# Attention and token MLP on one core: masked Q evacuation in place of padded Q weights, two extra matmuls a period, new load order and tail

## Chip, cores and metric

One core of one Trainium2 chip. The metric is device time of the whole kernel in microseconds (us), median of several executions; lower is better. Launch-to-launch spread of the kernel before is about 0.3%.

## The reference

`x` is [1, 2048, 512] bf16. Layernorm gives `xn`; the result is `x + A(xn) + B(xn)`.

```python
def A(x, wqkv, wo):                 # 32 heads of 16
    q, k, v = split(x @ wqkv)
    p = softmax((q @ k.T) * 16 ** -0.5)
    return (p @ v) @ wo

def B(x, w1, b1, w2, b2):           # MLP over the tokens, F = 1376
    h = layernorm(x)
    u = gelu(h.T @ w1 + b1)
    return (u @ w2 + b2).T
```

The scores have 32 x 2048 x 2048 elements, and each of them needs an exp.

## The kernel before

Work is recorded into one stream for each engine by a Python loop over 512 *periods*. A period handles one group: 128 keys of four heads against 512 queries. Sixteen periods (all 2048 keys) are a *block*; 32 blocks cover 8 groups of heads and 4 blocks of queries. In each period TensorE does 4 score matmuls (q times k), 4 PV matmuls (p times v) of an earlier period, and a few *extra* matmuls of everything else; ScalarE does two exps. To *evacuate* is to copy a matmul's result out of PSUM, the memory that TensorE writes to, into SBUF, the working memory. Code and diffs here are shortened (an instruction stands for the call that records it, `...` for what is left out); the whole kernel is printed below.

```python
while True:
    if period < NGRP:
        score_group(period)                 # TensorE: 4 matmuls, 32 rows each (0.61 us together at half clock)
        exp_pair(2 * period)                # ScalarE: [128, 1024], PSUM -> SBUF
        exp_pair(2 * period + 1)
    ...                                     # PV of a period before; after 16 of them the block's epilogue
    budget = EXTRA_BUDGET if period < END else 1e9        # 3.0
    while bank_q:                           # one spare PSUM bank (EX_BANK), so one task at a time
        tk = bank_q[0]
        ...
        if tk.req == 0.0:                   # a step without matmuls (evacuation): ends the period's extras
            tk.advance()
            if period < END: break
            continue
        if budget >= tk.req or budget >= EXTRA_BUDGET:
            budget -= tk.req
            tk.advance()
        else: break
```

Tasks: `kt` (K projections, 4 chunks of 4 matmuls), `qt` (Q projection of one block, 4 matmuls), `ut` (first MLP product, 11 tasks of 16 matmuls, then gelu, whose tanh runs on ScalarE), `yt` (second product, 16 tasks of 11), `op` (output projection, 8 matmuls for 128 tokens).

Heads lie 16 rows apart and the score matmuls' tiles 32 (32*128 in their profile rows). So the 32 heads' Q weights were copied into a padded array with zeros, once for even and once for odd heads:

```python
def qt_block(b, bk, evac_eng="dve"):
    qb, G = divmod(b, NG)
    for ct in range(NCT):
        matmul(bank(bk), lhsT=wq_pad[:, ct, G, :], rhs=xnT[:, ct, 512*qb:512*(qb+1)], ...)
    evac(evac_eng, QT[:, b % NQS, :], bank(bk), ...)
```

GpSimd filled `wq_pad` (4 memsets, 8 copies) between its layernorm steps in the start stage.

The softmax here doesn't subtract the row's maximum and nothing guards it: scores larger than these inputs give would overflow.

## Time and profile before

| | before |
|---|---|
| median of 12 | 1041.68 us (1040.19 to 1043.09) |
| span of the profiled run | 1040.5 us |
| ScalarE busy / TensorE busy | 93% / 86% |
| start to first exp | 43.8 us |
| first exp to end of last exp | 981.6 us |
| end of last exp to end | 15.1 us |
| mean granted TensorE clock | 0.705 |

ScalarE's exps are the chain, so only start, tail and the breaks between exps can be saved. The views are shown and worked out in the prediction; one row of the page is added here. It gives the granted TensorE clock in 40 slices of 26 us, in tenths of full speed:

```profile
PEclk9966887897889999955557755555555955555558
```

From slice 18 on the row is mostly at 5, half clock (0.57 on the mean from 450 to 1000 us). This is the part of the kernel where only attention is left.

### The profile page before, as it was taken

The numbers are of one execution on the slowest core, as the hardware profiler recorded it, in microseconds if no ns is written. First come the engines' busy times: TensorE is split into PE (matmuls) and PEld (weight loads), VectorE is DVE, ScalarE is ACT, GpSimd is POOL, SyncE is SP. The second block draws the span as 40 slices with busy tenths as digits, with TensorE's granted clock in tenths as the row PEclk, the third lists the DMA queues.
The fourth block names the chain that finished last, engine by engine and source line by source line (L and its number), as shares of the span: only waits on it lengthen the run. The fifth ranks groups of instructions, "written<-read, shape, count | busy, mean of one in ns | idle before, by whom it ended". The sixth has DMA issues, their size and how long they took to land.

```text
span 1040.5 us, 11570 instructions
## 1 busy us (share of the span) xinstructions
PE 895.5 (86%) x4833; PEld 210.2 (20%) x4896; DVE 295.0 (28%) x476; ACT 967.2 (93%) x1065; POOL 75.8 (7%) x116
## 2 busy tenths in 40 slices
PE   5777888888889999999988898888998899888995
PEld 2211222221222222211112211111111211111111
DVE  6654433343332223322211222221022222102214
ACT  3698999999999999999999999999999999999994
POOL 6431000000000000000000000000000000000000
PEclk9966887897889999955557755555555955555558
DMA  5020201011012111100000000000000000000000
GB/s 141 19 43 21 48 21 41 21 27 30 1 29 53 35 29 43 28 0 1 1 1 11 11 1 1 1 1 1 0 1 6 16 1 1 1 1 1 1 1 20
DMA packets 54372, 18.31 MB, mean 18 GB/s; under 512 B 49200, under 2 KB 53808, under 8 KB 54320
## 3 DMA queue, kind: packets, MB, share of 16 engines
q1 hardware_dynamic: 54320, 17.58, 7.1%
q8 instruction: 38, 0.62, 0.2%
q14 instruction: 14, 0.11, 0.0%
HBM read 15.47 MB, written 2.10 MB: 17 GB/s over the span
## 4 chain that ended last, share of the span: by engine, by line
ACT 77%; PE 15%; DVE 4%; issue 1%; POOL 1%; DMA 1%; ACTq 0%; SPq 0%
ACT pT L597 77%; PE ps L588 4%; PE ps L383 3%; PE ps L607 2%; PE ps L468 2%; DVE stats L323 1%; DVE big L338 1%; PE ps L400 1%; POOL mv L329 1%; PE ps L514 1%; DMA x_sb<-in_A_x_dram 1%; PE ps L369 1%; ACT ga_sb L483 1%; DVE mv L325 0%; POOL mv L327 0%
## 5 line engine op out<-in xcount | busy, mean ns | idle before, releaser
L597 ACT ACTIVATE pT<-ps 128x1024 bf16<-128x1024 f32 x1024 | 946.3, 1242 | 32.8 <-PE ps L588 32.7
L588 PE MATMUL ps<-QT,KT 32*128 32x512 bf16 x2048 | 483.5, 513 | 97.2 <-ACT pT L597 62.0
L607 PE MATMUL ps<-pT,V 128*32 128x512 bf16 x2048 | 264.0, 517 | 2.2 <-DVE OT L546 1.9
L588 PEld LDWEIGHTS ps<-QT,KT 32*128 32x128 bf16 x2048 | 93.5, 96 | 509.5 <-ACT pT L597 460.2
L546 DVE COPY OT<-ps 128x512 f32<-128x512 f32 x32 | 22.1, 692 | 436.9 <-PE ps L607 436.8
L559 DVE RECIPROCAL denb<-denb 128x128 f32<-128x128 f32 x128 | 110.3, 915 | 0.9
L569 POOL TENSOR_TENSOR oT<-OT,denb 128x512 bf16<-128x512 f32 x31 | 39.3, 1267 | 881.6 <-DVE denb L559 881.6
L607 PEld LDWEIGHTS ps<-pT,V 128*32 128x32 bf16 x2048 | 52.9, 99 | 171.2 <-issue 167.9
L468 PE MATMUL ps<-big,w1blk 128*128 128x512 bf16 (+1 forms) x165 | 54.5, 436 | 2.8 <-issue 2.1
L383 PE MATMUL ps<-xnT,wq_pad 128*128 128x512 bf16 x101 | 43.2, 558 | 7.8 <-issue 7.8
L495 PE MATMUL ps<-gT,w2blk 128*128 128x512 bf16 (+1 forms) x165 | 47.3, 387 | 2.3 <-issue 1.9
L514 PE MATMUL ps<-wo_pad,oT 128*128 128x512 bf16 x115 | 36.0, 415 | 2.0 <-issue 1.8
L377 DVE CAST QT<-ps 128x512 bf16<-128x512 f32 x31 | 21.4, 692 | 36.2 <-PE ps L383 36.2
L500 DVE SCALAR_TENSOR_TENSOR big<-ps,x_sb 128x512 f32<-128x512 f32 x16 | 11.1, 691 | 66.8 <-PE ps L495 66.8
L473 DVE TENSOR_SCALAR u_sb<-ps,b1col 128x512 f32<-128x512 f32 (+1 forms) x11 | 8.2, 750 | 73.4 <-PE ps L468 73.4
L527 DVE TENSOR_TENSOR osb<-ps,big 128x512 bf16<-128x512 f32 x16 | 11.1, 691 | 58.0 <-PE ps L514 55.4
L376 ACT ACTIVATE xnT<-ps 128x512 bf16<-128x512 bf16 x16 | 9.5, 594 | 16.1 <-PE ps L348 16.1
L554 DVE STREAM_SHUFFLE denb<-OT 128x512 f32<-128x512 f32 x32 | 23.1, 722 | 0.0
L369 PE MATMUL ps<-xnT,wqkv_sb 128*128 128x512 bf16 x61 | 17.9, 412 | 3.8 <-DVE KT L377 3.2
L348 PE MATMUL ps<-ident,big 128*128 128x128 bf16 x64 | 7.0, 237 | 15.9 <-DVE big L338 15.9
L468 PEld LDWEIGHTS ps<-big,w1blk 128*128 128x128 bf16 (+1 forms) x176 | 14.1, 106 | 29.1 <-issue 21.4
L383 PEld LDWEIGHTS ps<-xnT,wq_pad 128*128 128x128 bf16 x128 | 12.9, 121 | 27.7 <-issue 24.5
(44 smaller groups left out, 209.6 us busy)
## 6 DMA issues: line engine op xcount, KB each, us to landing
w1blk<-in_B_w_dram SPq DMA_DIRECT2D x10, 512.0 KB, 4.1
w2blk<-in_B_w_dram SPq DMA_DIRECT2D x16, 320.0 KB, 3.3
out_dram<-osb SPq DMA_DIRECT2D x16, 128.0 KB, 1.7
wqkv_sb<-in_A_wqkv_dram SPq DMA_DIRECT2D x1, 1536.0 KB, 6.6
x_sb<-in_A_x_dram SPq DMA_DIRECT2D x3, 512.0 KB, 8.5
wo_pad<-in_A_wo_dram SPq DMA_DIRECT2D x8, 64.0 KB, 2.0
w2blk<-in_B_w_dram SPq DMA_DIRECT2D x16, 24.0 KB, 1.8
w1blk<-in_B_w_dram SPq DMA_DIRECT2D x1, 384.0 KB, 4.0
```

Of the source, the lines that this page charges most:

```text
L369: sc.add("pe", lambda e, ct=ct: e.matmul(bank(bk), lhsT=wqkv_sb[:, ct, D + 128 * T: D + 128 * T + 128], rhs=xnT[:, ct, 512 * c:512 * (c + ...
L383: sc.add("pe", lambda e, ct=ct: e.matmul(bank(bk), lhsT=wq_pad[:, ct, G, :], rhs=xnT[:, ct, 512 * qb:512 * (qb + 1)], start=(ct == 0), sto ...
L468: sc.add("pe", lambda e, st=st: e.matmul(bank(EX_BANK)[0:m, :], lhsT=w1blk[:, slot, st, 0:m], rhs=h_sb[:, st, :], start=(st == 0), stop=(s ...
L495: sc.add("pe", lambda e, ft=ft, m=m: e.matmul(bank(EX_BANK), lhsT=w2blk[0:m, slot, ft, :], rhs=gT[0:m, ft, :], start=(ft == 0), stop=(ft = ...
L514: sc.add("pe", lambda e, G=G: e.matmul(bank(EX_BANK), lhsT=oT[:, par, G, 128 * sti:128 * (sti + 1)], rhs=wo_pad[:, G, :], start=(G == 0), ...
L546: sc.add("dve", lambda e: e.tensor_copy(OT32[:, eb, :], bank(PV_BANK)), reads=[("bank", PV_BANK)], writes=[("OT32", eb)])
L554: sc.add("dve", lambda e: e.stream_shuffle(denb[:, eb, :], OT32[:, eb, :], [16] * 32), reads=[("OT32", eb)], writes=[("denb", eb, c) for c ...
L559: sc.add("dve", lambda e, cs=cs: e.reciprocal(denb[:, eb, cs], denb[:, eb, cs]), reads=[("denb", eb, c)], writes=[("denb", eb, c)])
L569: sc.add("pool", lambda e: e.tensor_tensor(oT[:, qb % 2, G, :], OT32[:, eb, :], denb[:, eb, :], ALU.mult), reads=[("OT32", eb)] + [("denb" ...
L588: sc.add("pe", lambda e, r=r, bk=bk: e.matmul(bank(bk), lhsT=KT[32 * r:32 * r + 32, T, 128 * kt:128 * (kt + 1)], rhs=QT[32 * r:32 * r + 32 ...
L597: sc.add("act", lambda e: e.activation(pT[:, buf, :], ps[:, s_ * 1024:(s_ + 1) * 1024], ACTF.Exp, scale=0.25), reads=[("bank", 2 * s_), (" ...
L607: sc.add("pe", lambda e, r=r, buf=buf, off=off: e.matmul(bank(PV_BANK)[32 * r:32 * r + 32, :], lhsT=V17[:, off:off + 32], rhs=pT[:, buf, 5 ...
```

## The change

Intent: halve the Q projection matmuls, spread the extra work more thinly, start earlier, and shorten the tail.

```diff
-EXTRA_BUDGET = 3.0
+EXTRA_BUDGET = 2.0
-        wq_pad = sb("wq_pad", [128, NCT, NG, 128], BF16)
+        qmask = sb("qmask", [128, 2], F32)        # 1 on 16 rows, 0 on 16; and the opposite
 ...
+        ld_x(0, 1); ld_x(1, 2); ld_w(2)            # V weights
+        ld_x(2, 4); ld_x(4, 8); ld_w(1)            # K weights
+        ld_x(8, 12); ld_x(12, 16); ld_w(0)         # Q weights   (before: x(0,1), all weights, the rest of x)
 ...
+        def qt_proj(qb, T, bk):                    # one projection for two blocks
+            for ct in range(NCT):
+                matmul(bank(bk), lhsT=wqkv_sb[:, ct, 128*T:128*(T+1)], rhs=xnT[...])
+            for e_ in range(2):
+                b = 8 * qb + 2 * T + e_
+                tensor_scalar(QT[:, b % NQS, :], bank(bk), qmask[:, e_:e_+1], None, ALU.mult)   # VectorE
 ...
-            ng = NG - 1 if lastqb else NG
+            ng = NG - 2 if lastqb else NG          # last query block: two groups are left for the tail
 ...
+        def tail_epilogue(b):
+            for sti in range(4): final_pre(qb, sti)            # group 6 into banks 0..3, under the shuffle
+            stream_shuffle(denb, bank(PV_BANK), [16] * 32)      # straight out of PSUM, no copy
+            recip_mult(0)                                       # reciprocal, multiply, final matmul
+            for c in range(1, 4):
+                recip_mult(c)
+                final_store(4 * qb + c - 1, c - 1)              # the store runs one chunk behind
+            final_store(4 * qb + 3, 3)
 ...
                     tk.advance()
+                    if tk.req == 0.0 and period < END:          # evacuate in the period of the last matmul
+                        tk.advance()
+                        break
```

## The prediction

> **What bounds the kernel now.** I read four views in this order: the page's chain of work that ended last with the costliest groups, ScalarE's own timeline, TensorE's timeline around one gap, and VectorE's timeline at the start and at the end.
>
> ```profile
> ACT 77%; PE 15%; DVE 4%; issue 1%; POOL 1%; DMA 1%; ACTq 0%; SPq 0%
> ...
> L597 ACT ACTIVATE pT<-ps 128x1024 bf16<-128x1024 f32 x1024 | 946.3, 1242 | 32.8 <-PE ps L588 32.7
> ...
> L383 PE MATMUL ps<-xnT,wq_pad 128*128 128x512 bf16 x101 | 43.2, 558 | 7.8 <-issue 7.8
> ```
>
> The exp on ScalarE (L597) is the chain. It ran 1024 times and was idle only 32.8 us, and all of that for scores (L588). TensorE's 86% busy share is therefore no bound by itself; what counts is where the scores come late. ScalarE's timeline shows that as breaks in its runs of exps:
>
> ```profile
> 514.39 29.44 ACT L597 ACTIVATE pT<-ps 128x1024 bf16<-128x1024 f32 x32 [0.86 <-PE ps L588]
> 544.68 12.94 ACT L597 ACTIVATE pT<-ps 128x1024 bf16<-128x1024 f32 x14 [0.86 <-PE ps L588]
> 558.05 1.94 ACT L597 ACTIVATE pT<-ps 128x1024 bf16<-128x1024 f32 x2 [0.43 <-PE ps L588]
> 560.54 44.10 ACT L597 ACTIVATE pT<-ps 128x1024 bf16<-128x1024 f32 x48 [0.55 <-PE ps L588]
> 605.50 29.44 ACT L597 ACTIVATE pT<-ps 128x1024 bf16<-128x1024 f32 x32 [0.86 <-PE ps L588]
> ```
>
> A run of 2 takes 1.94 and one of 32 takes 29.44, so the pitch is (29.44 - 1.94)/30 = 0.917 us, and 1024 of them cost 939. Each break costs its idle time plus 0.11 of drain (1.94 - 2 x 0.917). First exp at 43.78, last one done at 1025.4, span 1040.5: so 43.8 of start, 981.6 of exps (939, some 4.5 for the 11 tanh, the rest breaks) and 15.1 of tail. The breaks sort by what TensorE did just before them: early, up to 80 us, 3 of them, 3.0 us; in the stage of the first MLP product (80 to 295 us) 21 breaks, 15.3 us; from 450 us on 16 breaks of 0.86, each after a Q projection (L383), 16 x 0.96 = 15.4; and three pairs of 0.43 and 0.55, where output projections start, 3.5. Sum 37.
>
> Why they exist, seen at one of the pairs on TensorE:
>
> ```profile
> 162.40 1.46 PE L468 MATMUL ps<-big,w1blk 128*128 128x512 bf16 x3
> 163.79 0.61 PE L588 MATMUL ps<-QT,KT 32*128 32x512 bf16 x4
> 164.34 0.62 PE L607 MATMUL ps<-pT,V 128*32 128x512 bf16 x4
> 164.89 1.46 PE L468 MATMUL ps<-big,w1blk 128*128 128x512 bf16 x3
> ```
>
> This is the slow clock (granted 0.5). One period is 4 scores, 4 PV and the extras that the schedule slips in: 0.55 + 0.55 + 3 x 0.46 = 2.49 us, against 1.83 for the two exps that it feeds. At full clock the same three extras fit (no break from 300 to 450 us). With 4 extras, a Q projection, it is some 2.9: hence the 0.96 per Q projection.
>
> [...]in stretches of 0.5 us the granted clock rises at 560.40, 802.74 and 1014.37[...].
> [...]the layernorm's tensor_scalar takes 0.38 us alone and 1.01 while GpSimd clears wq_pad.
> [...]plain evacuation of 128x512 0.692 us, tensor_scalar of the same size (L473) 0.750. So a mask on the way out is nearly free.
>
> **The change, part by part.**
> *Q projection.* One projection now serves two blocks, and two masked evacuations on VectorE split it. Matmuls of this kind fall from 128 to 64, evacuations stay 32 (31 on VectorE before, all 32 now, 0.7 each, off the path). In the new order of instructions the projections stand in every second block; those in the long attention-only stretch, where the clock is slow, are 5 (blocks 19, 21, 23, 27, 29; those in 17 and 25 stand among output projections). 5 x 0.96 = 4.8 in place of 15.4: -10.6.
> *Two extras a period in place of three.* At slow clock: 0.55 + 0.55 + 2 x 0.46 = 2.03, that is 0.20 over the exps, and the first 0.12 is slack. [...]it should still wake the clock, [...]some 2.5 periods, 0.4 us a start in place of 1.2. [...]it stays warm. The MLP stage has 11 gaps of two empty periods in the new order. A gap puts the clock back[...] (I take 70%, before it was nearly always): 0.7 x (6 starts x 0.4 + 2 K projections x 1.5 + 3 Q projections x 1.1) = 6.1, plus 1.9 at its first block: 8.0 in place of 15.3, -7.3. Output projections: two starts of 0.4 and four short bursts at the end, 2.4 in place of 3.5, -1.1. I charge +0.7 for a second product that now and then falls cold on its one-extra period, and +0.8 because a Q projection now holds the extra bank for two evacuations (0.7 longer) before the next extras. Exp stage: -10.6 - 7.3 - 1.1 + 1.5 = -17.5.
> *Start.*
>
> ```profile
> 8.17 0.69 DVE L323 BATCH_NORM_STATS2 stats<-x_sb 128x6 f32<-128x512 bf16 x1 [4.37 <-DMA x_sb<-in_A_x_dram]
> ...
> 9.00 0.38 DVE L338 TENSOR_SCALAR big<-x_sb,mv 128x512 bf16<-128x512 bf16 x1
> ...
> 10.15 1.01 DVE L338 TENSOR_SCALAR big<-x_sb,mv 128x512 bf16<-128x512 bf16 x1
> ```
>
> The second x tile waited 4.37 behind 1536 KB of weights. It now goes ahead of them, and weights come in three parts in order of need: -4.3. Three memsets of wq_pad go (3 x 0.63 = 1.9 of VectorE), but TensorE is cold and saturated there, so I count 1.0 only. The last layernorm waits 3.6 us under the memset of wo_pad at 33.4; that memset stays where it is. Start: -5.3, first exp near 38.5.
> *Tail.*
>
> ```profile
> 1029.14 0.69 DVE L527 TENSOR_TENSOR osb<-ps,big 128x512 bf16<-128x512 f32 x1 [0.48 <-PE ps L537]
> 1029.75 0.68 DVE L520 TENSOR_TENSOR big<-ps,big 128x512 f32<-128x512 f32 x1
> ...
> 1032.32 0.69 DVE L527 TENSOR_TENSOR osb<-ps,big 128x512 bf16<-128x512 f32 x1 [0.70 <-PE ps L537]
> ```
>
> VectorE's chain from 1025.89 to 1038.16 is 12.27 us. Gone: the copy out of PSUM (0.74), the last residual add (0.6, now earlier) and four waits for the final matmul (0.48 + 3 x 0.70 = 2.58), since each store now follows the next reciprocal and multiply. Left: shuffle 0.75, four times 1.29, three stores at 0.61 and one of 0.69: 8.4, so -3.8; I take 3.7, as the last stores wait a little for the two output buffers (1.7 us from issue to landing). Two groups are left for the end in place of one, but the first of them is multiplied under the shuffle.
> Sum: 5.3 + 17.5 + 3.7 = 26.5, so 1041.75 - 26.5 = 1015.
>
> **The rivals.** (a) Two extras never wake the clock. [...]Then the MLP's 88 periods pay 0.2 each, 17.6, until some projection wakes it: about 1028. (b) Two extras wake it, but do not hold it, or the two evacuations and two-slot bank make new waits: +5 to +8, about 1022. (c) The gaps of the slow clock are only an accompaniment, and halving the Q projections gives nothing as the K projections' and evacuations' waits take their place: 1030. Against it: each break after 450 us has a Q projection before it and nothing else. (d) The memsets' full 1.9 is gained and gaps rarely cool the clock: 1009.
>
> **Range and chances.** Start and tail are well founded (9.0, give or take 1.5); the exp stage is 17.5 with some 6 either way, mostly downward through the clock. 8 in 10: 1008 to 1024. The line of 2% is 1020.9; (a), half of (b) and (c) lie beyond it. Faster 0.77, within 2% 0.22, slower 0.01.
>
> **What would show it.** Right: first exp at 38 to 39; breaks of 0.86 only in every second block after 450 us; at starts of two extras, two or three breaks near 0.2 and then a warm clock; no L520 add and no wait of 0.7 for TensorE in the tail, which is 11.4 us long. Wrong: a clock of 0.5 through the stage of the MLP with a break of 0.2 in each period; breaks with the release by the masked evacuation; or a first exp after 41.

## The result and the profile after

1019.03 us, median of 8 (1015.42 to 1020.05), against 1041.68. The ratio is 0.978 (95% interval 0.9769 to 0.9792). Ratios here are the mean time of one kernel's fast runs over that of the other's of the same rounds, so they are not quite the ratio of the quoted medians. The predicted time was 1015, the range 1008 to 1024.

Span 1018.1, that is 22.4 less. The same checkpoints of ScalarE's timeline, before and after:

| stretch | before | after | difference | predicted |
|---|---|---|---|---|
| start to first exp | 43.78 | 40.84 | -2.9 | -5.3 |
| first exp to exp 41 | 41.30 | 41.86 | +0.6 | 0 |
| exp 41 to exp 297 (first MLP product) | 254.1 | 249.2 | -4.9 | -7.3 |
| exp 297 to end of last exp | 686.2 | 675.2 | -11.0 | -10.2 |
| tail | 15.1 | 11.1 | -4.0 | -3.7 |

(Exp 297 of the kernel before has no break at it; its start is worked out as 293.34 + 50 x 0.917 from the break before it. The start differs from run to run; see a3. The -10.2 is the prediction's -10.6 for the Q projections, -1.1 for output projections, +1.5 of charges.)

From the page of the changed kernel:

```profile
PEclk9767898987788999997996855555555955555566
...
L619 ACT ACTIVATE pT<-ps 128x1024 bf16<-128x1024 f32 x1024 | 946.8, 1277 | 18.5 <-PE ps L610 16.8
...
L387 PE MATMUL ps<-xnT,wqkv_sb 128*128 128x512 bf16 x55 | 21.8, 530 | 2.8 <-issue 2.8
```

ScalarE's idle time before exps went from 32.8 to 18.5. By the clock record of the two traces, the scores that ended a break of over 0.15 us ran at half clock in 43 of 46 breaks before (30.1 of 32.2 us) and in 19 of 22 after (13.5 of 15.2). The projection group shows 55 matmuls against 101 (some records are missing in both: 64 and 128 were built). ScalarE's timeline, late part:

```profile
683.32 58.77 ACT L619 ACTIVATE pT<-ps 128x1024 bf16<-128x1024 f32 x64 [0.86 <-PE ps L610]
742.95 117.55 ACT L619 ACTIVATE pT<-ps 128x1024 bf16<-128x1024 f32 x128 [0.86 <-PE ps L610]
861.35 58.77 ACT L619 ACTIVATE pT<-ps 128x1024 bf16<-128x1024 f32 x64 [0.86 <-PE ps L610]
```

The runs between breaks are now mostly 64 or 128 exps long, two or four blocks, where most were 32. From 600 us on there are five breaks of 0.86, at blocks 19, 21, 23, 27 and 29, as foretold.

TensorE's timeline at the start of the first MLP task:

```profile
82.06 0.61 PE L610 MATMUL ps<-QT,KT 32*128 32x512 bf16 x4
82.60 0.62 PE L629 MATMUL ps<-pT,V 128*32 128x512 bf16 x4
83.15 1.03 PE L471 MATMUL ps<-big,w1blk 128*128 128x512 bf16 x2
84.11 0.61 PE L610 MATMUL ps<-QT,KT 32*128 32x512 bf16 x4
...
86.17 0.53 PE L610 MATMUL ps<-QT,KT 32*128 32x512 bf16 x4
```

Periods start at 82.06, 84.11 and 86.17: 2.055 us each at the slow clock (granted 0.5; 2.03 was predicted), and the clock rises to full at 86.5 (the 0.53 and the shorter matmuls that follow it). So two extras do wake it. The loss of 0.22 a period (2.055 against two exps of 0.917) need not show in the idle column: the drain of an exp (0.11) hides half of it, and the view doesn't split a run at an idle time as short as the rest (0.11). This row of ScalarE's timeline shows none, but the run is longer than its count allows:

```profile
99.92 18.93 ACT L619 ACTIVATE pT<-ps 128x1024 bf16<-128x1024 f32 x20
```

Twenty exps should take 19 x 0.917 + 1.02 = 18.44; the run took 0.49 more (the starts of two of its exps come 0.31 and 0.22 late; before the second, ScalarE idled 0.12). Whoever sums idle times misses this part.

### The profile page after: what moved, and what is told of

Its sections match the earlier page's. It is cut to its first block, busy times and chain, and to the rows that moved or that the text cites. A ratio compares the mean times of both kernels' runs of the same rounds, so it can differ in the third digit from the quotient of the medians.

```text
span 1018.1 us, 11428 instructions
## 1 busy us (share of the span) xinstructions
PE 860.1 (84%) x4770; PEld 197.2 (19%) x4832; DVE 294.5 (29%) x476; ACT 966.6 (95%) x1064; POOL 70.7 (7%) x110
## 4 chain that ended last, share of the span: by engine, by line
ACT 80%; PE 13%; DVE 4%; POOL 1%; issue 1%; DMA 0%; SPq 0%; ACTq 0%
ACT pT L619 79%; PE ps L610 4%; PE ps L629 2%; PE ps L387 1%; PE ps L471 1%; DVE stats L329 1%; PE ps L409 1%; DVE big L344 1%; PE ps L375 1%; POOL mv L335 1%; PE ps L517 1%; ACT ga_sb L486 1%; DMA x_sb<-in_A_x_dram 0%; PE ps L354 0%; DVE mv L331 0%
## 5 line engine op out<-in xcount | busy, mean ns | idle before, releaser
L619 ACT ACTIVATE pT<-ps 128x1024 bf16<-128x1024 f32 x1024 | 946.8, 1277 | 18.5 <-PE ps L610 16.8
L610 PE MATMUL ps<-QT,KT 32*128 32x512 bf16 x2048 | 463.6, 494 | 117.8 <-ACT pT L619 91.5
L629 PE MATMUL ps<-pT,V 128*32 128x512 bf16 x2048 | 257.7, 505 | 2.4 <-DVE OT L553 1.9
L565 DVE RECIPROCAL denb<-denb 128x128 f32<-128x128 f32 x124 | 107.0, 915 | 0.9
L471 PE MATMUL ps<-big,w1blk 128*128 128x512 bf16 (+1 forms) x160 | 56.7, 432 | 4.4 <-issue 2.9
L498 PE MATMUL ps<-gT,w2blk 128*128 128x512 bf16 (+1 forms) x160 | 54.1, 405 | 3.3 <-issue 1.9
L517 PE MATMUL ps<-wo_pad,oT 128*128 128x512 bf16 x105 | 38.5, 441 | 5.5 <-issue 3.2
L394 DVE TENSOR_SCALAR QT<-ps,qmask 128x512 bf16<-128x512 f32 x32 | 22.6, 747 | 18.9 <-PE ps L387 18.9
L387 PE MATMUL ps<-xnT,wqkv_sb 128*128 128x512 bf16 x55 | 21.8, 530 | 2.8 <-issue 2.8
L560 DVE STREAM_SHUFFLE denb<-OT 128x512 f32<-128x512 f32 x31 | 22.4, 723 | 0.0
L375 PE MATMUL ps<-xnT,wqkv_sb 128*128 128x512 bf16 x61 | 20.0, 458 | 2.6 <-DVE KT L383 1.5
L335 POOL TENSOR_TENSOR mv<-mv,mhalf 128x1 f32<-128x1 f32 x32 | 18.2, 568 | 2.7
L409 PE MATMUL ps<-wqkv_sb,xnT 128*128 128x512 bf16 x62 | 18.1, 419 | 0.1
```

The lines of the kernel that those rows point to most:

```text
L335: sc.add("pool", lambda e: e.tensor_tensor(mv[:, i, 2:3], mv[:, i, 1:2], mhalf[:], ALU.pow), reads=[("mv", i), ("mhalf",)], writes=[("mv", ...
L375: sc.add("pe", lambda e, ct=ct: e.matmul(bank(bk), lhsT=wqkv_sb[:, ct, D + 128 * T: D + 128 * T + 128], rhs=xnT[:, ct, 512 * c:512 * (c + ...
L387: sc.add("pe", lambda e, ct=ct: e.matmul(bank(bk), lhsT=wqkv_sb[:, ct, 128 * T:128 * (T + 1)], rhs=xnT[:, ct, 512 * qb:512 * (qb + 1)], st ...
L409: sc.add("pe", lambda e, ct=ct: e.matmul(bank(bk), lhsT=xnT[:, ct, 128 * t:128 * (t + 1)], rhs=wqkv_sb[:, ct, 2 * D:3 * D], start=(ct == 0 ...
L471: sc.add("pe", lambda e, st=st: e.matmul(bank(EX_BANK)[0:m, :], lhsT=w1blk[:, slot, st, 0:m], rhs=h_sb[:, st, :], start=(st == 0), stop=(s ...
L498: sc.add("pe", lambda e, ft=ft, m=m: e.matmul(bank(EX_BANK), lhsT=w2blk[0:m, slot, ft, :], rhs=gT[0:m, ft, :], start=(ft == 0), stop=(ft = ...
```

## The experiments

Twelve kernels, in three lots, each lot on one chip with its own runs of the kernel before (1044.02, 1042.0 and 1042.39 us). To compare I use ratios to the kernel before; one percent of it is 10.4 us. The 95% interval of a ratio is about 0.002 to either side, 2 us: by time alone, a difference of 2 us from the change (a3, a4, and nearly c1) isn't clear of noise, and the traces have to decide.

| run | edit to the changed kernel | median us | ratio to before | mean clock |
|---|---|---|---|---|
| the change itself | | 1019.03 | 0.978 | 0.74 |
| a1 | three extras | 1032.72 | 0.9899 | 0.689 |
| a2 | one projection a block | 1026.31 | 0.9847 | 0.767 |
| a3 | loads of before | 1022.3 | 0.9798 | 0.746 |
| a4 | tail of before (wrong result) | 1022.15 | 0.98 | 0.754 |
| c2 | tail of before, mended | 1025.41 | 0.9844 | 0.747 |
| b1 | + two idle matmuls a period | 1004.92 | 0.9646 | 0.961 |
| b2 | + the same from block 16 only | 1012.15 | 0.9711 | 0.938 |
| c1 | + one idle matmul a period | 1016.09 | 0.9755 | 0.81 |
| b3 | kernel *before* + two idle matmuls | 1011.7 | 0.9712 | 0.976 |
| b4 | clearing of wo_pad moved | 1015.65 | 0.9749 | 0.741 |
| c3 | b1 and b4 together | 1001.49 | 0.9614 | 0.962 |
| c4 | c3 + second layernorm in two steps | 997.24 | 0.9572 | 0.966 |

The theory: ScalarE's exps are the floor, and the breaks between them come from TensorE at half clock, where a period with two extra matmuls or more takes longer than two exps (2.055 us with two, against 1.83). The change gains by making fewer such periods. The rival: TensorE's amount of work, or waits for evacuations, make the breaks. One part of the change, that a task now evacuates in the period of its last matmul, was undone in no run.

### Undoing one part each

**a1, three extras.**

```diff
-EXTRA_BUDGET = 2.0
+EXTRA_BUDGET = 3.0
```

> The changed kernel with three extra matmuls a period again in place of two (all else kept). Theory (starts at the slow clock cost ScalarE 0.66 us a period with three extras and 0.22 with two): the eleven restarts of the first MLP product and the starts of the output projections cost about 0.6 us more each; about 1026 us, with breaks in pairs of 0.43 and 0.55 back in the profile. Rival (the cost of a restart does not depend on the number of extras[...]): within 1 us of 1019.

Measured: 12 us slower than the change by ratio (0.0119), nearly twice what I expected. Two causes are in ScalarE's timeline: the stage of the first MLP product (exp 41 to exp 297) alone is 7.5 us longer, 256.7 against 249.2, which is what I expected for all; the rest is late. The pairs of breaks are back, also at each short burst of output projections at the end:

```profile
974.16 1.94 ACT L619 ACTIVATE pT<-ps 128x1024 bf16<-128x1024 f32 x2 [0.43 <-PE ps L610]
976.65 7.44 ACT L619 ACTIVATE pT<-ps 128x1024 bf16<-128x1024 f32 x8 [0.55 <-PE ps L610]
984.52 1.94 ACT L619 ACTIVATE pT<-ps 128x1024 bf16<-128x1024 f32 x2 [0.43 <-PE ps L610]
987.01 9.27 ACT L619 ACTIVATE pT<-ps 128x1024 bf16<-128x1024 f32 x10 [0.55 <-PE ps L610]
```

And the MLP is done in block 12 in place of block 16, so the Q projections of blocks 13 and 15 fall into the stretch at half clock (breaks of 0.86 at 454.8 and 514.4 us). The rival is out, since the restarts of that stage cost what the theory said. So two extras do two things: restarts get cheaper (the 7.5 us), and the clock stays up longer since the work lasts longer (mean clock 0.74 in the change, 0.689 in a1).

**a2, one projection a block.**

```diff
-            for e_ in range(2):
+            for e_ in only:                      # (e_,): one masked evacuation a projection
...
-                    sched_list.append((P(b - 1, 1), 0, "qt", (qb, T)))
+                    for e_ in range(2): sched_list.append((P(b' - 1, 1), 0, "qt", (qb, T, e_)))
```

> The changed kernel, but each block projects its own Q again (four matmuls and one masked evacuation a block, so 128 projection matmuls in place of 64). Theory (every lone Q projection at the slow clock holds ScalarE up by 0.96): eleven or twelve more breaks of 0.86 in the attention-only stretch and one to three more earlier, some 12 us: about 1031 us. Rival (projections are hidden anyway and what helped was the rest): within 2 us of 1019.

Measured: 7.0 us slower by ratio (0.0067; its runs scatter from 1023 to 1029). After 515 us it has 12 breaks of 0.86 or so and one of 0.43, in place of 6 in all; eleven were to be added, seven were (blocks 18, 20, 22, 24, 26, 28 and 30). The direction is right, the size too large: with two extras the MLP lasts into block 16 here (542.6 us) and output projections follow, and the clock, at 1.0 but for one stretch from 326 to 579 us (slices 14 to 22 of its row are at 9), covers the projections of blocks 13 to 16.

**a3, the old loads.**

```diff
-        ld_x(0, 1); ld_x(1, 2); ld_w(2); ld_x(2, 4); ld_x(4, 8); ld_w(1); ld_x(8, 12); ld_x(12, 16); ld_w(0)
+        ld_x(0, 1); <all of wqkv in one transfer>; ld_x(1, 2); ld_x(2, 4); ld_x(4, 8); ld_x(8, 12); ld_x(12, 16)
```

> The changed kernel with the loads of before: the first x tile, then all weights in one transfer, then the rest of x. Theory: the first exp moves back by 3.2 us (the first VectorE evacuation of V was at 11.91 in the changed kernel and at 15.07 before), about 1022 us, first exp at 44. Rival (the gain at the start is from the removed clearing of the padded weights, not from the loads): first exp at 41 to 42.

Measured: first exp at 43.17 in place of 40.84. But the first exp moves from run to run with unchanged start code: 39.42 in a4, 40.69 to 40.87 in the change, b1, b2, c1 and c2, 41.15 in a1. The clock record shows a reason: the change has a stretch of half clock from 35.3 to 38.7 us, just after TensorE waited 3.1 us for VectorE, the other five from 40.69 up have one near there too, and a4 has none before its first exp. Neither have a3 and b3 (the start of the kernel before, 42.86). (The second slice of the clock row, 25 to 51 us, is at 7 or 8 in those six and at 9 in these three.) Like with like, the order of loads is worth 43.17 - 39.42 = 3.75 us, up to 0.7 of it a late landing in a3 (VectorE starts on tile 1 at 8.99, in b3 at 8.32), and nothing is seen of the rest (the removed filling of the padded weights, the first Q evacuation on VectorE). The exp stage was the same, 965.2 us against 966.2. By ratio it is 1.9 us.

**a4 and c2, the old tail.** In a4 I left the last output projections where the change puts them, in block 30. With one group more they then read a group that isn't written yet, in the program's order: the result was wrong (relative error 0.19). The timing of the tail isn't touched by that, but c2 repeats it with right results.

```diff
-            ng = NG - 2 if lastqb else NG
+            ng = NG - 1 if lastqb else NG
-            stream_shuffle(denb, bank(PV_BANK), ...)
+            epilogue_copy(b); stream_shuffle(denb, OT32[:, eb, :], ...)
-            (stores one chunk behind)
+            for c in range(4): recip_mult(c); final_store(4 * qb + c, c)
 c2 also:  last output projections from block 31, period 8 on, three extras there
```

> The changed kernel with the tail of before: copy out of PSUM first, one final group of matmuls, each store straight after its own multiply, one group more in the output projections of the last block. Theory: tail 4 us longer, from last exp to end 15.1 in place of 11.05, about 1023 us. Rival (the tail's gain is only that of the one residual add): 1 us longer.

> The old tail once more, now with right results: the last output projections start in block 31 as before the change, with three extras there, all residual adds ahead of the tail, then the copy out of PSUM and store after store. Theory: tail from last exp to end 14 to 15 us in place of 11.05, 1022 to 1023 us. Rival (the tail makes no difference as stores are hidden): 1019 us.

Measured: in a4 14.8 us from the last exp to the end, in c2 16.6, in the change 11.1. By ratio a4 is 2.1 us slower than the change and c2 6.7. (a4's profile is only 1.6 us longer, though its tail is 3.7 longer, as its first exp came 1.4 earlier, see a3, and its exp stage was 0.7 shorter.) In c2 the exp stage is 966.3, as in the change (966.2), and so is the first exp (40.87), so of the 5.6 us between the two profiles 5.5 are the tail; its last residual add stands in front of the copy and waits:

```profile
1009.22 0.69 DVE L523 TENSOR_TENSOR big<-ps,big 128x512 f32<-128x512 f32 x1 [1.94 <-PE ps L517]
1009.83 0.68 DVE L553 COPY OT<-ps 128x512 f32<-128x512 f32 x1
```

So c2's tail is 1.5 us worse than that of the kernel before, and I take 4 us, the difference of the two traces, for the tail's worth. In the changed kernel's tail, the stores follow without any wait for TensorE, and the last two run back to back:

```profile
1012.69 0.68 DVE L530 TENSOR_TENSOR osb<-ps,big 128x512 bf16<-128x512 f32 x1
...
1014.47 1.48 DVE L530 TENSOR_TENSOR osb<-ps,big 128x512 bf16<-128x512 f32 x2
```

### Is it the clock?

These runs add work and change nothing else. Two matmuls whose result nobody reads go into the spare bank in each period that has no extras:

```diff
+            n_pe = len(sc.streams["pe"])
 ...
+            if 20 <= period < NGRP and len(sc.streams["pe"]) == n_pe:      # b2: 256 in place of 20; c1: one in place of two
+                for _ in range(2):
+                    sc.add("pe", lambda e: e.matmul(bank(EX_BANK), lhsT=wqkv_sb[:, 0, 0:128], rhs=xnT[:, 0, 0:512],
+                                                    start=True, stop=True), writes=[("bank", EX_BANK)])
```

> The changed kernel with two idle matmuls (into the spare PSUM bank, result never read) in every period from 20 on that has no extra work. Results stay right. Theory (what is left of the breaks after 85 us comes from a TensorE at half clock): the clock stays at 1.0 from 90 us to the end, the breaks go, some 15 us less: about 1004 us. Rival (breaks come from the amount of TensorE work or from waits for evacuations): more matmuls, so the same or slower, 1019 or above.

> As the run with idle matmuls everywhere, but only from period 256 (block 16, about 515 us) on. Theory: the five breaks of 0.86 at the lone Q projections and those at the last output projections go, some 6 us less: about 1013 us, first half as in the changed kernel. Rival: no gain.

> The kernel before (padded weights, one projection a block, three extras, old tail) with the same two idle matmuls in every period without extra work from period 20 on. Theory (halving the projections and lowering the extras only avoid what a slow clock does): nearly all of its 33 us of breaks after 85 us go too, about 1010 us, faster than the changed kernel. Rival (fewer matmuls are what counts): it stays at 1042 or gets slower.

Measured: 1004.92, 1012.15 and 1011.7 us, each within 2 us of what the theory said. With some 450 matmuls more (weight loads of the built kernel: 5284 against 4832), TensorE makes ScalarE wait less (in b1 8.8 us before exps in place of 18.5). The clock row of b1, then of b3, and ScalarE's timeline of b3 (the kernel *before*, with all its Q projections) from 440 us on:

```profile
PEclk9767898999999999998999999999999999999998
```

```profile
PEclk9967999999999999999999999999999999999997
```

```profile
438.14 555.55 ACT L597 ACTIVATE pT<-ps 128x1024 bf16<-128x1024 f32 x605
```

In that stretch the 16 lone Q projections and the output projections' starts cost nothing any more: 605 exps in one run (the row starts where the stretch that I looked at starts; it ends with the last exp), at 555.55/605 = 0.918 us each. The rival is refuted: the same number of projections, more TensorE work, and no break. b3 is faster than the changed kernel by 0.7% (0.9712 against 0.978), with none of its edits.

It follows how the change gained in the exp stage: not by saving TensorE work as such, but by avoiding what a slow clock makes of it. With the clock kept up (mean 0.961 in b1, 0.976 in b3), the change's other edits gain nothing there: from first exp to the end of the last it is 952.7 us in b1 and 950.8 in b3. By ratio b1 is still 6.9 us faster (0.0066). That equals the change's start and tail (2.9 + 4.0), but in part by luck: in the two profiles it is 4.5, of which 2.2 are the start (b1 has the slow stretch in it, b3 has not), 4.1 the tail, and -1.8 the exp stage (b1 keeps two breaks there, 1.08 at 325.1 and 0.43 at 472.4, both at half clock).

**c1, one idle matmul.**

> As the run with idle matmuls everywhere (1004.9 us), but one idle matmul a period in place of two. [...]Theory[...]: it does not hold, the attention-only stretch goes back to 0.5 in most of its windows and most of the five breaks of 0.86 return; 1014 to 1019 us. Rival (any work in the gap is enough): as with two, 1005 us.

Measured: 1016.09. Its clock row, and rows of ScalarE's timeline from 600 us on:

```profile
PEclk9767899898899999998989977556775966566776
```

```profile
619.81 58.94 ACT L619 ACTIVATE pT<-ps 128x1024 bf16<-128x1024 f32 x64 [0.22 <-PE ps L610]
679.61 1.94 ACT L619 ACTIVATE pT<-ps 128x1024 bf16<-128x1024 f32 x2 [0.86 <-PE ps L610]
...
739.25 117.83 ACT L619 ACTIVATE pT<-ps 128x1024 bf16<-128x1024 f32 x128 [0.25 <-PE ps L610]
857.93 58.88 ACT L619 ACTIVATE pT<-ps 128x1024 bf16<-128x1024 f32 x64 [0.85 <-PE ps L610]
917.67 1.94 ACT L619 ACTIVATE pT<-ps 128x1024 bf16<-128x1024 f32 x2 [0.86 <-PE ps L610]
```

In 600:690, 690:780 and 870:960 us the mean clock is 0.62, 0.64 and 0.61, where the change had 0.52, 0.50 and 0.50: it holds for part of the time only. Three of the five breaks stayed at 0.85 or more, the other two fell to a quarter. One idle matmul a period (mean clock 0.81 over the run) doesn't keep the clock up, two do (0.961 in b1). So half measures buy little: by ratio 2.6 us (0.978 - 0.9755), where two idle matmuls give 14 (0.978 - 0.9646). Nor do short waits alone keep it up: from 90 us to the last exp of the kernel before and of the changed one TensorE never waited longer than 1.04 us, and still their mean clock from 450 to 1000 us is 0.57 and 0.64. What decides when the clock falls was not shown.

### What is left

**b4, the clearing of the output weights later.**

```diff
-        late_consts()                     # GpSimd clears wo_pad right after the first stage
+        (in the loop)  if period == P(2, 0): late_consts(1)
```

> The changed kernel, with the clearing of the padded output weights on GpSimd and their loads moved from the end of the start stage to block 2. Theory (the last layernorm is locked out for 3.6 us by that clearing): first exp 3.2 us earlier, about 37.6, and 1016 us. Rival (something else would hold the first exp): no change. The bench of the start then also has no gap that lets TensorE cool, worth up to 1 us more.

Measured: first exp at 36.36, 4.5 us earlier than in the profile of the change, and 3.2 us less by ratio (0.0031). Against a4's start, which has no stretch of half clock either, it is 3.1 earlier: so about 3.1 are the lock-out and the other 1.4 the slow stretch. First a row of the change's VectorE timeline, then the same one after the move:

```profile
30.29 3.61 DVE L344 TENSOR_SCALAR big<-x_sb,mv 128x512 bf16<-128x512 bf16 x1 [0.77 <-POOL mv L335]
```

```profile
30.68 0.41 DVE L346 TENSOR_SCALAR big<-x_sb,mv 128x512 bf16<-128x512 bf16 x1 [0.77 <-POOL mv L337]
```

The same instruction takes 3.61 under GpSimd's memset and 0.41 without it. It is two memsets, 3.55 us together; the second began at 31.95, when VectorE had stood waiting since 30.29, and still went first.

**c3 and c4, together.** c3 is b1 with b4. c4 also splits the second layernorm:

```diff
-            for t in range(NT): yield 0.0; ln_tile(t, 1)
+            for t in range(NT + 1):
+                yield 0.0
+                if t < NT: ln_stats(t, 1)
+                if t > 0: ln_norm(t - 1, 1)
```

> The changed kernel with two idle matmuls a period and the clearing of the padded output weights moved to block 2. Theory: the two gains (14 and 3.4 us) add, as one lies in the exp stage and one ahead of it: about 1001 us. Rival (the moved clearing's loads or GpSimd work disturb the stage, or the gains overlap): 1003 to 1005 us.

> The same, and the second layernorm written in two steps, so that VectorE takes the statistics of the next tile while GpSimd works on the previous one. Theory (the five breaks before 85 us, 5 us in all, are VectorE's backlog: each tile of the second layernorm waits 1.0 us for GpSimd): most of them go, about 997 us. Rival (they come from the K projections' single PSUM bank): no change against the run without it.

Measured: 1001.49 and 997.24 us, both right by their results. The gains add up. ScalarE's timeline up to 85 us, first of c3, then of c4:

```profile
36.38 7.56 ACT L621 ACTIVATE pT<-ps 128x1024 bf16<-128x1024 f32 x8 [1.50 <-PE ps L612]
44.50 3.87 ACT L621 ACTIVATE pT<-ps 128x1024 bf16<-128x1024 f32 x4 [0.56 <-PE ps L612]
49.26 22.11 ACT L621 ACTIVATE pT<-ps 128x1024 bf16<-128x1024 f32 x24 [0.88 <-PE ps L612]
72.22 3.77 ACT L621 ACTIVATE pT<-ps 128x1024 bf16<-128x1024 f32 x4 [0.86 <-PE ps L612]
77.39 13.39 ACT L621 ACTIVATE pT<-ps 128x1024 bf16<-128x1024 f32 x14 [1.40 <-PE ps L612]
```

```profile
36.41 7.44 ACT L624 ACTIVATE pT<-ps 128x1024 bf16<-128x1024 f32 x8 [1.51 <-PE ps L615]
44.53 25.77 ACT L624 ACTIVATE pT<-ps 128x1024 bf16<-128x1024 f32 x28 [0.68 <-PE ps L615]
71.16 19.36 ACT L624 ACTIVATE pT<-ps 128x1024 bf16<-128x1024 f32 x21 [0.86 <-PE ps L615]
```

After the first exp, c3 has four breaks (0.56, 0.88, 0.86, 1.40) and c4 two (0.68, 0.86). From first exp to exp 41 that is 2.6 us (41.0 against 38.4), of the 4.8 by which c4's exp stage is shorter; where the other 2.2, later on, come from was not looked into. c4 is 4.3% faster than the kernel before. Its exps run from 36.41 to 985.36, which is 949 us, against 939 for the exps themselves and some 4.5 for the tanh between them.

## Why the prediction was right, and where it was off

The sum of 26.5 was 4 us too large, inside the range: the start and the stage of the first MLP product gave 2.4 us less each, the rest together 0.5 more.

*ScalarE is the floor and breaks are what can be saved*: right. c4, with nearly no breaks (5.6 us of idle time before exps), comes to 949 us of exp stage, 10 above the count times the pitch.

*A lone Q projection at the slow clock costs 0.96*: right. Five of them remained, in the blocks named, each a break of 0.86, and a warm clock takes them away (b2, mean clock 0.938; b3, 0.976, for the kernel before). But the sum *gave it too much*. I put all eleven that vanish (16 to 5) down to the halving. a2 shows 7.0 us for it; by the blocks, seven are due to halving (7 x 0.96 = 6.7) and the other four, in blocks 13 to 16, to the longer life of the MLP under two extras. The stretch as a whole came to -11.0 where I had -10.2, as the two errors are the same microseconds under another name.

*Two extras wake the clock and hold it*: right, though only an estimate beforehand (2.055 us a period, woken after two such periods at the first start; mean clock 0.94 from 300 to 450 us; rival (a) is out). *A restart costs 0.4, and only 70% of the gaps cool the clock*: this step failed in size. In the trace of the change all twelve gaps of that stage cooled it. Successive drops lie 20.5 us apart, at 168.4, 188.9, 212.8 (this one 23.9 on), 233.3, 253.7 and 274.2; why at these distances was not shown. With 1.0 in place of 0.7, the term 0.7 x 8.7 is 8.7, with the 1.9 of the first block 10.6; measured, the stage lost 10.1 over its floor (249.2 less 256 x 0.917 and eleven tanh of 0.4), and 1.4 in the break just before it. The 2.6 from 8.0 to 10.6 are about the 2.4 us by which the -7.3 was too much.

*Start -5.3*: failed in size, -2.9 (-3.4 without the slow stretch, from b3's 42.86 to a4's 39.42). The first exp, at 40.84, missed its sign of 38 to 39 and lies just under the 41 that was to show the prediction wrong. I moved the whole chain by the 4.3 us that tile 1 no longer waits. The VectorE timeline of the change has two waits in its place:

```profile
6.49 0.69 DVE L329 BATCH_NORM_STATS2 stats<-x_sb 128x6 f32<-128x512 bf16 x1 [1.31 <-DMA x_sb<-in_A_x_dram]
...
11.91 0.69 DVE L383 CAST V<-ps 128x512 bf16<-128x512 f32 x1 [1.85 <-PE ps L409]
```

Tile 2 waits for its own transfer, and then VectorE for a TensorE that has four matmuls of 0.43 a tile to do (1.91 for the four at 8.16; from 11.93 on four take 1.03); from the evacuation of V's tile 1 on (11.91 against 15.07) both kernels keep the same pace. Of the 1.0 for the memsets nothing is seen (a3 against b3); that the same wait swallowed it is likely, but not shown.

*Tail -3.7*: right, -4.0 by the traces; shown by a4 and c2, which move it back. No wait for TensorE, no residual add (L520 before), 11.1 us.

*Rival (b), new waits by the two evacuations*: seen, but small: in the list of waits TensorE waits some 6 us in all for the masked evacuation, and one break of ScalarE after the start follows such a wait (0.60 at 281.3, after TensorE waited 0.41 at 279.7, at half clock). The 0.90 at 331.9 is a Q projection at half clock: its masked evacuation begins only after the scores that end the break.

*A mask on the way out is nearly free*: right, the masked evacuation took 0.747 us against 0.692 plain.

## What to carry to other kernels

When an engine is the floor, list its breaks and what the feeding engine did just before them, and divide each run by its count: losses shorter than the pipeline's drain (0.11 us here) hide in the length of runs and not in the idle column (0.49 in a run of 20 exps). If the feeder is TensorE and its clock row is at half, try first to keep the clock up with idle matmuls in the empty periods: on the kernel before that gained 30 us (b3, 1 - 0.9712), where the whole restructuring gained 23, and it shows at once which of the planned savings are only symptoms of the slow clock. An undo of one part of a change measures that part with all the others present, so parts that share a gain (fewer projections, longer warm stretch) must not be added up from the trace of before alone.
